# Fused sigmoid attention and MLP mixer on one core: tile 2 of two lots kept and done together with the next lot's, by seven products

## The chip, the cores and the metric

The kernel runs on one core of a Trainium2 chip. The time is device microseconds of one execution: the median of the runs of the kernel before is 340.74 us (three runs, 340.58 to 341.35). The engines are named as in the profile: PE is TensorE (matmuls), PEld its weight loads, DVE is VectorE, ACT is ScalarE, POOL is GpSimd, SP is SyncE, which here issues DMAs.

## The reference

```python
# q, k, v: (8, 12, 448, 64) float32; S = 448
scores = (1 / sqrt(64)) * q @ k.transpose(0, 1, 3, 2) - log(S)
attn = 1 / (1 + exp(-scores)) @ v                  # per batch and head
x = attn.transpose(0, 2, 1, 3).reshape(8, 448, 768)
xt = x.transpose(0, 2, 1)
u = x + (relu(xt @ w_tok1) @ w_tok2).transpose(0, 2, 1)   # w_tok1 (448, 256)
out = u + relu(u @ w_ch1) @ w_ch2                          # w_ch1 (768, 1536)
```

Four pieces follow each other for each of the eight batches: attention, the token mixer (448 to 256 to 448), the first channel product (768 to 1536) and the second one (1536 to 768).

## The kernel before, in words

**Stages.** Work is written out by hand in one order (`manual_schedule`: nothing is moved), three batches deep. A cycle is one batch `b` and one unit `u` of four heads, so three cycles make a batch. In the steady part (`steady`, b = 3 to 7) a cycle holds the seven score tiles of (b, u) (`qk`, L187: PE writes one of two PSUM buffers, ACT takes the sigmoid, L194), attention times values of the cycle before (`av`, L218), the token mixer of the cycle before that (`tok_tail` L277, `tok1` L296, `ytrans` L316), and pieces of the second channel product of `lot = b - 2`. At the end of u = 2 stands the whole first channel product of batch b - 1 (`sevens`, L516), on which ACT and DVE work as well.

**Array modes.** Scores, values and the "split" products run the array as four 64x64 quarters; `tok1`, `ytrans`, `sevens` and the "plain" products run it whole (128x128). In each cycle the 64x64 work comes first and one stretch of 128x128 work ends it.

**Seven products.** Tiles are 128 tokens: tiles 0, 1, 2 of a lot are whole, tile 3 has 64 tokens. `ch2_seven` does two tiles by Strassen's seven products over halves of the contraction and of the output columns, each of six blocks of 128 (a block is one 128x128 matmul of 384 columns, or one step of four 64x64 ones). Products 1, 6, 7, 4 pile up in that order in one PSUM bank, 2 in a second, 5 and 3 in a third tile that has the second one's bank. After each product its `end` (L843, DVE) adds the bank into an output tile, so a product that goes on in a bank waits for the `end` of the one before it there. Sums of weights that the products need are made by DVE (`sums`, L803). The output is stored by SP after products 3 (first tile) and 4 (second).

**Who does what, before.** u = 0: products 1 and 2 split (`two_jobs`), 6 and 5 plain. u = 1: 7 and 3 split, 4 plain. u = 2: tile 3 as a split (`last_split`, L671), then tile 2 alone (`ch2_pair`, 24 blocks: 14 split at L387 and 10 plain at L652), then `sevens`. A run that is split in two turns has a DVE copy of one element (`turn_over`, L854) between the turns.

**Banks and buffers.** PSUM banks 0 and 1 ("Y") are used in turn by `av`, `tok_tail`/`tok1` and `ytrans`, banks 2 and 3 ("X") by the lot's products; each use waits until DVE or ACT has emptied the bank. DVE empties `av` by two casts (L227), `ytrans` by two adds into `xu` (L326). The SBUF tag `parts` is a ring of four buffers that holds the outputs of tiles 0 and 1 and the six ACT copies of `sevens` (`pt_ab` and `pt_c`, L537) in the order in which they are asked for; a copy into a buffer that held an output waits until that output is stored. `h2` (the hidden layer), `diffs`, `outs`, `raw_q`, `rel_k` and `rel_q` have one buffer each, `un` (u, tokens first) two.

**Token sums and relayouts.** `token_sums(b - 1)` (four DVE instructions, L459) makes the sums that `sevens` uses from its fifth step on. `through_dma` gives eight pieces for the next batch's k and q: three DVE copies (L129) and one DMA transpose on SP (L142), for k and then for q; `some(n)` does the next n of them, (0, 1) in u = 0 (`within`, `behind`), (3, 4) in u = 1. `utrans` (L343) is one more DMA transpose on SP, at the end of u = 1. `gated_loads` lets POOL wait for the q transpose and then load.

Of the kernel before, what the change touches and what calls it, by code (L numbers as in the profile page):

```python
# [9 lines left out]
FP16 = mybir.dt.float16  # L10
FP32 = mybir.dt.float32
# [10 lines left out]
NJ = 7  # L22
NP = 64
NU = 3
# [6 lines left out]
def kernel(  # L31
# [11 lines left out]
    nc = tc.nc  # L43

    B, H, S, E = q.shape
# [4 lines left out]
    NCB = CC // 128  # L50
# [216 lines left out]
    def tok_tail(b, u):  # L267

        h1_tile(b, u)
        tks[b] = [  # L270
            bank([128, 2, 2, 128], FP32, f"tk_{b}_{u}_{tcb}")[:, 0, :, :]
            for tcb in range(2)
        ]
        for tcb in range(2):
            part = slice(64 * tcb, 64 * tcb + 64)
            for g in range(2):
                nc.tensor.matmul(  # L277
                    out=tks[b][tcb][64 * g : 64 * g + 64],
                    lhsT=w1[part, 3, 128 * tcb + 64 * g : 128 * tcb + 64 * g + 64],
                    rhs=xn[b, u][part, :, 3, :],  # L280
                    start=True,
                    stop=False,
                )
# [177 lines left out]
    def ch1_seven(b, banks):  # L461
# [93 lines left out]
    outs = {}  # L555
    orow = out.rearrange("b (p j) d -> b j p d", j=NJ)

    AT_END = {
        (B - 2, 0): "raw_k",
        (B - 2, 1): "raw_q",  # L560
# [5 lines left out]
    def out_tile(b, t):  # L566
        if b == 0 and t < 2:
            outs[b, t] = out_0[:, D * t : D * t + D]
            return
        tag, bufs = ("outs", 1) if t == 2 else ("parts", 4)  # L570
        if (b, t) in AT_END:
            tag, bufs = AT_END[b, t], 2 if AT_END[b, t] == "raw_v" else 1
        outs[b, t] = pa.tile([128, D], FP32, tag=tag, bufs=bufs, name=f"o_{b}_{t}")
# [188 lines left out]
    class ch2_seven:  # L762

        CHAIN = {1: "X", 6: "X", 7: "X", 4: "X", 2: "Y", 5: "Z", 3: "Z"}

        def __init__(self, rows, sides, X, Y, Z, at_end=True):
            self.rows, self.ps, self.banks = rows, {}, {"X": X, "Y": Y, "Z": Z}
            b = rows[1][0]
            tag, bufs = ("tr_k", 2) if at_end else ("diffs", 1)
            hid = pa.tile(  # L770
                [128, 3, NCB // 2, 128], FP16, tag=tag, bufs=bufs, name=f"hid_{b}"
            )
            self.held = {n: hid[:, at, :, :] for at, n in enumerate((5, 6, 7))}
            if at_end:
                hid3 = pa.tile(
                    [128, NCB // 2, 128], FP16, tag="tr_q", bufs=2, name=f"hid3_{b}"
                )
                self.held[3] = hid3[:, :, :]
            (self.a11, self.a12), (self.a21, self.a22) = [
                (side[:, LOW, :], side[:, HIGH, :]) for side in sides  # L780
            ]
            self.held.setdefault(3, self.a12)
            self.weights = {1: self.a11, 2: self.a12, 4: self.a22}
            self.moving = {
                1: c2[:, LOW, D1],
                2: c2[:, HIGH, D1],
                3: c2[:, HIGH, D2],
                5: hsums[0],
                6: hsums[1],
                7: hsums[2],  # L790
                4: hsums[3],
            }
# [43 lines left out]
        def end(self, n):  # L836
            row, half = {1: (0, 0), 2: (0, 0), 6: (0, 1), 3: (0, 1)}.get(n, (1, int(n != 4)))
            b, t = self.rows[row]
            if (b, t) not in outs:
                out_tile(b, t)  # L840
            o = outs[b, t][:, DH * half : DH * half + DH].rearrange("s (u d) -> s u d", d=128)
            opens = n in (1, 6, 5, 4)
            nc.vector.tensor_tensor(  # L843
                out=o,
                in0=un[b][:, :, half, t, :] if opens else o,
                in1=self.ps[self.CHAIN[n]][:, 0:DH].rearrange("s (u d) -> s u d", d=128),
                op=ADD,
            )
            if n in (3, 4):
                store(b, t)  # L850

    def turn_over(ps):

        nc.vector.tensor_copy(out=turned[:, :], in_=ps[:, 0:1])  # L854

    def two_jobs(jobs):

        def step(turn, n):
            for r in range(2):
                ps, lhsT, rhs, opens, end = jobs[r ^ turn]  # L860
                part = slice(64 * r, 64 * r + 64)
                for m in (0, 64):
                    nc.tensor.matmul(  # L863
                        out=ps[m : m + 64, 0:DH],
                        lhsT=lhsT(n)[part, m : m + 64],
                        rhs=rhs(n)[part, :],
                        start=(opens and turn == 0 and n == 0),
                        stop=(turn == 1 and n == NCB // 2 - 1),
                        skip_group_check=True,
                    )  # L870

        def end():
            for job in jobs:
                job[-1]()

        turns = [
            [lambda t=t, n=n: step(t, n) for n in range(NCB // 2)] for t in range(2)
        ]
        return turns[0], lambda: turn_over(jobs[1][0]), turns[1], end
# [335 lines left out]
    def some(n):  # L1215
        for f in copies[:n]:
            f()
        del copies[:n]
# [83 lines left out]
    def more(n):  # L1302
        for f in extra[:n]:
            f()
        del extra[:n]
# [5 lines left out]
    def score(n=1):  # L1311
        for _ in range(n):
            qk(*next(scores))

    def steady(b, u):

        lot, before, ahead = b - 2, divmod(NU * b + u - 1, NU), divmod(NU * b + u - 2, NU)
        within, behind = (
            ((0, 0), (4, 2), (2, 0)) if b == NU else ((0, 1), (3, 4), (0, 0))
        )[u]  # L1320

        def run(steps, n):
            for f in steps[:n]:
                f()
            del steps[:n]

        at_bank[0] = X
        if u < 2:
            if u == 0:
                sides = [h2[lot][:, :, 128 * t : 128 * t + 128] for t in range(2)]  # L1330
                sevenfold[lot] = ch2_seven(
                    [(lot, 0), (lot, 1)], sides, X, X + 1, X + 1, at_end=False
                )
                sevenfold[lot].sums(0, 2)
            more((0, 3)[u])
            seven = sevenfold[lot]
            turn0, turn, turn1, end = two_jobs([seven.job(n) for n in ((1, 2), (7, 3))[u]])
            score(2)
            run(turn0, 6)
            turn()  # L1340
            at_bank[0] = Y
            av(*before, 0, 1)
            score()
            av(*before, 1, 5)
            score()
            av(*before, 5, NJ)
            xtrans_dma(*before)
            run(turn1, 2)
            score()
            run(turn1, 4)  # L1350
            end()
            if u == 0:
                if b + 1 < B:
                    nc.gpsimd.tensor_copy(out=gate[:, :], in_=outs[lot, 0][:, 0:2])
                    load(b + 1, "q", q, 0, NU)
                seven.sums(2, 4)
                more(1)
            score()
            some(within)
            at_bank[0] = Y  # L1360
            tok_tail(*ahead)
            tok1(*ahead, with_scores=True)
            for n in ((6, 5), (4,))[u]:
                seven.plain(n)
        else:
            ps = [bank([128, 512], FP32, f"c2_{lot}_3_{r}") for r in range(2)]
            steps, end = last_split(lot, ps)
            score(2)
            run(steps, 7)
            score()  # L1370
            run(steps, 5)
            send = end(put_off=True)
            some(within)
            score()
            at_bank[0] = Y
            av(*before, 0, 5)
            score()
            at_bank[0] = X
            turn0, turn1, rest = ch2_pair(lot, u, 7, loose=True)
            run(turn0, 3)  # L1380
            score()
            run(turn0, 4)
            turn_over(turn_bank[0])
            av(*before, 5, NJ)
            xtrans_dma(*before)
            send()
            token_sums(b - 1)
            score()
            run(turn1, 2)
            score()  # L1390
            run(turn1, 5)
            at_bank[0] = Y
            tok_tail(*ahead)
            score()
            tok1(*ahead, with_scores=True)
            rest()
            sevens(b - 1)
        at_bank[0] = Y
        ytrans(*ahead)
        if u == 1:  # L1400
            utrans(b - 1)
        some(behind)
        if u == (2 if b == NU else 1) and b < B - 1:
            gated_loads(b)

    for c in range(ONE_RUN, N_CYCLES):
# [100 lines left out]
```

## Time and profile before

| what | value |
|---|---|
| median of the runs | 340.74 us |
| the profiled execution, whole | 340.27 us |
| its span | 338.5 us |
| PE busy, share of the span | 332.2 us, 98% |
| DVE busy | 235.3 us, 70% |
| ACT busy | 212.7 us, 63% |
| one batch of the steady part (138.9 to 177.3 us, 177.3 to 215.6 us) | 38.4 and 38.3 us |

The profiled execution lies 0.47 us under the median; 1.77 us of it lie outside the span. A row of the timeline gives the start (us from the span's start), the time from the first start to the last end, the engine, the line, the operation, what it writes and reads, the shape and how many alike follow each other. A PE matmul's own duration is longer than the time until the next may start, so the pace is read from starts. For a DMA that SP issues, the row's duration is the time for which SP is taken by the issue, not the time until the data has landed.

### The profile page before, as it was taken

How to read it: one execution, taken by the hardware profiler on the slowest of the kernel's cores; microseconds unless marked ns; L12 is line 12 of the kernel's file. 1: busy time of each engine (PE TensorE's matmuls, PEld its weight loads, DVE VectorE, ACT ScalarE, POOL GpSimd, SP SyncE). 2: the span in 40 equal slices, each digit the busy share in tenths (PEclk: the TensorE clock that was granted, in tenths of full speed). 3: DMA queues.
4: the chain of work that ended last, by engine and by line, in shares of the span. 5: the costliest groups of instructions: out<-in, count | busy, mean ns of one | idle time of the engine just before them, and what ended most of it. 6: DMA issues, size and time to landing. Idle time of an engine off the chain costs nothing.

```text
span 338.5 us, 10318 instructions
## 1 busy us (share of the span) xinstructions
PE 332.2 (98%) x4436; PEld 242.9 (72%) x4436; DVE 235.3 (70%) x486; ACT 212.7 (63%) x272; POOL 61.7 (18%) x108
## 2 busy tenths in 40 slices
PE   8999999999999999999999999999999999999994
PEld 5655556555896679767896679766896679769852
DVE  2376466678998874877668774877768653976882
ACT  4996845388747885678647885678657895314200
POOL 8985380050031002020032001110010000000000
PEclk9999999999999999999999999999999999999999
DMA  8999999999999899989998899988993393028006
GB/s 128 162 160 202 207 178 203 175 175 234 186 179 194 158 171 203 182 125 179 186 190 133 152 151 215 201 123 163 195 179 65 67 171 85 2 56 186 4 13 196
DMA packets 103422, 51.91 MB, mean 153 GB/s; under 512 B 75473, under 2 KB 100305, under 8 KB 103377
## 3 DMA queue, kind: packets, MB, share of 16 engines
q1 hardware_dynamic: 77648, 28.84, 47.0%
q0 software_dynamic: 25264, 21.50, 42.4%
q10 hardware_dynamic: 464, 0.92, 1.0%
q8 instruction: 34, 0.56, 0.6%
q14 instruction: 12, 0.09, 0.1%
HBM read 43.45 MB, written 11.01 MB: 161 GB/s over the span
## 4 chain that ended last, share of the span: by engine, by line
PE 81%; DMA 11%; POOL 5%; DVE 1%; issue 1%; ACT 0%; ACTq 0%; POOLq 0%
PE c_ab L516 14%; PE c L816 10%; PE c_c L516 8%; PE qk L187 8%; PE xa L218 7%; PE c L863 6%; DMA raw_k<-in_k_dram 5%; PE tk L296 4%; PE yt L316 4%; PE c L586 4%; PE c L387 4%; DMA raw_v<-in_v_dram 3%; PE c L671 3%; DMA c<-in_moe_w_ch_dram 3%; PE c L652 2%; POOL raw_q L118 2%
## 5 line engine op out<-in xcount | busy, mean ns | idle before, releaser
L194 ACT ACTIVATE att<-qk,att_bias 128x896 f16<-128x896 f32 x168 | 155.9, 1012 | 37.8 <-PE qk L187 36.7
L187 PE MATMUL qk<-tr_q,tr_k 64*64 64x448 f16 x672 | 60.8, 357 | 0.3 <-DVE tr_k L179 0.2
L516 PEld LDWEIGHTS <-c 128*128 128x128 f16 x504 | 48.4, 98 | 1.1 <-issue 0.3
L218 PE MATMUL xa<-att,raw_v 64*64 64x448 f16 x644 | 40.6, 349 | 0.0
L187 PEld LDWEIGHTS <-tr_k 64*64 64x64 f16 x672 | 25.3, 104 | 18.7 <-issue 11.5
L516 PEld LDWEIGHTS <-sum 128*128 128x128 f16 x378 | 36.3, 98 | 0.0
L227 DVE CAST xu<-xa 128x448 f16<-128x448 f32 x40 | 23.1, 619 | 18.3 <-PE xa L218 17.9
L537 ACT ACTIVATE pt_ab<-c_ab 128x896 f32<-128x896 f32 x21 | 19.2, 917 | 20.6 <-PE c_ab L516 20.6
L218 PEld LDWEIGHTS <-raw_v 64*64 64x64 f16 x672 | 21.9, 107 | 8.2 <-issue 0.4
L863 PE MATMUL c<-c,h 64*64 64x384 f16 x360 | 24.6, 323 | 0.0
L1136 POOL COPY gate<-tr_q 128x2 f16<-128x2 f16 x6 | 1.1, 184 | 121.9 <-DMA tr_q<-rel_q 121.9
L326 DVE TENSOR_TENSOR xu<-xu,yt 128x448 f16<-128x448 f16 x38 | 21.8, 615 | 0.0
L539 ACT ACTIVATE h<-c_ab 128x896 f16<-128x896 f32 x7 | 6.4, 917 | 24.4 <-PE c_ab L516 24.4
L296 PE MATMUL tk<-xn,w 128*128 128x256 f16 x156 | 21.2, 274 | 0.1
L546 DVE TENSOR_TENSOR h<-pt_ab,c_ab 128x896 f16<-128x896 f32 x14 | 15.2, 1083 | 8.6 <-PE c_ab L516 8.6
L546 DVE TENSOR_TENSOR h<-pt_c,c_c 128x448 f16<-128x448 f32 x21 | 12.9, 616 | 11.7 <-PE c_c L516 11.6
L310 ACT ACTIVATE h<-tk 128x256 f16<-128x256 f32 x42 | 14.2, 405 | 9.9 <-PE tk L296 9.9
L316 PE MATMUL yt<-w,h 128*128 128x448 f16 x88 | 20.3, 353 | 0.0
L843 DVE TENSOR_TENSOR o<-un,c 128x384 f32<-128x384 f16 x32 | 17.4, 551 | 4.0 <-PE c L816 4.0
L816 PEld LDWEIGHTS <-hid 128*128 128x128 f16 x132 | 12.9, 98 | 8.0
L516 PE MATMUL c_ab<-diffs,c 128*128 128x224 f16 x168 | 18.4, 259 | 0.0
L118 POOL DMA_DIRECT2D raw_k<-in_k_dram x26 | 16.8, 661 | 8.0 <-DMA c<-in_moe_w_ch_dram 5.6
(132 smaller groups left out, 574.4 us busy)
## 6 DMA issues: line engine op xcount, KB each, us to landing
out_dram<-o SPq DMA_DIRECT2D x41, 192.0 KB, 3.3
c<-in_moe_w_ch_dram POOLq DMA_DIRECT2D x3, 1152.0 KB, 11.6
raw_k<-in_k_dram POOLq DMA_DIRECT2D x10, 336.0 KB, 6.6
raw_q<-in_q_dram POOLq DMA_DIRECT2D x10, 336.0 KB, 5.6
raw_v<-in_v_dram POOLq DMA_DIRECT2D x10, 336.0 KB, 8.2
raw_q<-in_q_dram POOLq DMA_DIRECT2D x16, 112.0 KB, 5.9
raw_k<-in_k_dram POOLq DMA_DIRECT2D x16, 112.0 KB, 6.9
out_dram<-o SPq DMA_DIRECT2D x15, 96.0 KB, 2.4
```

Source lines behind the costliest of these rows:

```text
L118: nc.gpsimd.dma_start(out=dst.rearrange("p u hi j e -> p (u hi) (j e)"), in_=heads.rearrange("h (p j) e -> p h (j e)", j=NJ),)
L187: nc.tensor.matmul(out=ps[64 * g : 64 * g + 64, hi, 0:S], lhsT=tr[b, "k"][64 * hi : 64 * hi + 64, u, j, 64 * g : 64 * g + 64], rhs=tr[b, " ...
L194: nc.scalar.activation(out=att[b, u, j][:, :, :], in_=ps[:, :, 0:S], func=SIGMOID, bias=bias_t[:, :], scale=att_scale,)
L218: nc.tensor.matmul(out=ps[g][64 * hi : 64 * hi + 64, 0:S], lhsT=raw[b, "v"][64 * g : 64 * g + 64, u, hi, j, :], rhs=att[b, u, j][64 * g : ...
L227: nc.vector.tensor_copy(out=xu(b)[:, u, g, 0:S], in_=ps[g][:, 0:S])
L296: nc.tensor.matmul(out=ps[tcb], lhsT=w1[rows, t, cols], rhs=xn[b, u][rows, :, t, :], start=(t == 0 and not with_scores), stop=(t == (2 if ...
L316: nc.tensor.matmul(out=ps[:, 0:S], lhsT=h1[b, u][:, tcb, g, :], rhs=w2[:, tcb, :, :], start=(tcb == 0), stop=(tcb == 1),)
L326: nc.vector.tensor_tensor(out=x, in0=x, in1=ps[:, 0:S], op=ADD)
L516: nc.tensor.matmul(out=ps[:, g, p, :], lhsT=weights[n][:, d, 128 * cb : 128 * cb + 128], rhs=moving[n][:, d, :], start=(n in (1, 5, 2) and ...
L546: nc.vector.tensor_tensor(out=shaped(dst), in0=shaped(parts[gs, which]), in1=ps, op=ADD)
L816: nc.tensor.matmul(out=ps[:, 0:DH], lhsT=self.weights[n][:, k, :], rhs=self.moving[n][:, k, :], start=(n in (1, 2, 5) and k == 0), stop=(k ...
L863: nc.tensor.matmul(out=ps[m : m + 64, 0:DH], lhsT=lhsT(n)[part, m : m + 64], rhs=rhs(n)[part, :], start=(opens and turn == 0 and n == 0), ...
```

## The change

For lots 2 and 4 (worked on in b = 4 and b = 6; "late") tile 2 is not done. Its hidden values and its piece of `un` are copied aside by DVE (`late`, `un_late`), and one batch later (b = 5 and b = 7; "paired") it is done together with tile 2 of lots 3 and 5 by seven products in place of `ch2_pair`.

- In a late batch the seven products of tiles 0 and 1 are dealt out anew: u = 0 has 1 and 2 split and 6 plain; u = 1 has 5 and 7 split, with `tok_tail` and `tok1` put into the second turn after two of its six steps; u = 2 has 3 and 4 split, ahead of tile 3 and of the values. The `within` and `behind` counts become (0, 1), (3, 1), and three pieces in u = 2 after the turn; `gated_loads` moves to u = 2. `token_sums` stays ahead of tile 3.
- In a paired batch u = 2 has two `sums` ahead of tile 3, then products 1 and 2 split, two more `sums`, 6 plain, `token_sums`, and 5, 7, 3, 4 plain. The sums are kept in `h2` itself.
- The two outputs of the pair lie in `raw_q` and `rel_k`, not in `outs` or the ring.

```diff
+    LATE_TILE = {4: 2, 6: 4}
+    PAIRED = {b + 1: lot for b, lot in LATE_TILE.items()}
...
+        if t == 2 and late:
+            tag, bufs = "raw_q" if b in LATE_TILE.values() else "rel_k", 1
...
+    def late_pair(lot):
+        free = h2[lot]
+        return ch2_seven(
+            [(PAIRED[lot + 2], 2), (lot, 2)],
+            [h2[PAIRED[lot + 2], "late"], free[:, :, 256:384]],
+            X,
+            X + 1,
+            X + 1,
+            at_end=False,
+            held={
+                5: free[:, LOW, 0:128],
+                6: free[:, HIGH, 0:128],
+                7: free[:, LOW, 128:256],
+                3: free[:, HIGH, 128:256],
+            },
+        )
...
+        if b in LATE_TILE:
+            within, behind = ((0, 1), (3, 1), (0, 0))[u]
...
-            turn0, turn, turn1, end = two_jobs([seven.job(n) for n in ((1, 2), (7, 3))[u]])
+            pair = ((1, 2), (5, 7) if b in LATE_TILE else (7, 3))[u]
+            turn0, turn, turn1, end = two_jobs([seven.job(n) for n in pair])
...
             run(turn1, 2)
             score()
+            split_run = u == 1 and b in LATE_TILE
+            if split_run:
+                at_bank[0] = Y
+                tok_tail(*ahead)
+                tok1(*ahead, with_scores=True)
             run(turn1, 4)
+            if split_run:
+                score()
             end()
...
-            for n in ((6, 5), (4,))[u]:
+            for n in ((6,), ())[u] if b in LATE_TILE else ((6, 5), (4,))[u]:
                 seven.plain(n)
+        elif b in LATE_TILE:
+            turn0, turn, turn1, end = two_jobs([sevenfold[lot].job(n) for n in (3, 4)])
+            score(2)
+            run(turn0, 6)
+            turn()
+            some(3)
+            at_bank[0] = Y
+            av(*before, 0, 2)
+            score()
+            run(turn1, 4)
+            score()
+            run(turn1, 2)
+            end()
+            av(*before, 2, 5)
+            score()
+            av(*before, 5, NJ)
+            xtrans_dma(*before)
+            token_sums(b - 1)
+            at_bank[0] = X
+            ps = [bank([128, 512], FP32, f"c2_{lot}_3_{r}") for r in range(2)]
+            steps, end = last_split(lot, ps)
+            run(steps, 4)
+            score()
+            run(steps, 3)
+            score()
+            run(steps, 3)
+            score()
+            run(steps, 2)
+            end()
+            late = pa.tile([128, NCB, 128], FP16, tag="outs", bufs=1, name=f"late_{lot}")
+            nc.vector.tensor_copy(out=late[:, :, :], in_=h2[lot][:, :, 256:384])
...
+            nc.vector.tensor_copy(out=un_late[lot][:, :, :, :], in_=un[lot][:, :, :, 2, :])
+            h2[lot, "late"] = late
             at_bank[0] = Y
             tok_tail(*ahead)
+            score()
             tok1(*ahead, with_scores=True)
+            sevens(b - 1)
         else:
+            both = late_pair(lot) if b in PAIRED else None
+            if both:
+                both.sums(0, 2)
...
             run(turn1, 5)
+            if both:
+                end()
+                both.sums(2, 4)
             at_bank[0] = Y
             tok_tail(*ahead)
             score()
             tok1(*ahead, with_scores=True)
-            rest()
+            if both:
+                both.plain(6)
+                token_sums(b - 1)
+                for n in (5, 7, 3, 4):
+                    both.plain(n)
+            else:
+                rest()
             sevens(b - 1)
...
-        if u == (2 if b == NU else 1) and b < B - 1:
+        if u == (2 if b == NU or b in LATE_TILE else 1) and b < B - 1:
             gated_loads(b)
```

## The prediction on record

> **What bounds the kernel now.** I read the page's busy lines first, then the stretches of one batch each, then PE's timeline through b = 4, then DVE, SP and ACT at the places that the change touches.
>
> ```profile
> PE 332.2 (98%) x4436; PEld 242.9 (72%) x4436; DVE 235.3 (70%) x486; ACT 212.7 (63%) x272; POOL 61.7 (18%) x108
> ```
> ```profile
> 138.90:177.30 38.40, 38.40 (x566) 29.92 (x564) 27.70 (x59) 26.92 (x36) 4.50 (x8) 1.00 1.02 175
> ...
> 330.00:338.50 8.50, 3.94 (x41) 2.35 (x39) 2.01 (x4) 0.48 (x1) 0.00 (x0) 0.90 0.70 196
> ```
>
> PE has no gap in a batch (38.40 of 38.40 us), so each matmul less is time, and each wait of PE is time too. PE timeline, u = 1 of b = 4 and on:
>
> ```profile
> 151.51 0.36 PE L187 MATMUL qk<-tr_q,tr_k 64*64 64x448 f16 x4
> 151.70 0.36 PE L277 MATMUL tk<-xn,w 64*64 64x256 f16 x4
> 151.99 0.83 PE L296 MATMUL tk<-xn,w 128*128 128x256 f16 x6
> 152.65 1.14 PE L816 MATMUL c<-hsum_b,h 128*128 128x384 f16 x6
> 153.63 0.92 PE L316 MATMUL yt<-w,h 128*128 128x448 f16 x4
> 154.48 0.57 PE L187 MATMUL qk<-tr_q,tr_k 64*64 64x448 f16 x8
> ...
> 162.84 1.79 PE L652 MATMUL c<-c,h 128*128 128x384 f16 x10
> 164.46 1.31 PE L516 MATMUL c_ab<-xu,c 128*128 128x224 f16 x12
> ```
>
> Paces from starts: a block is 0.162 us ((164.46 - 162.84)/10), a set of scores 0.19. The tail L277 takes 0.11, then PE waits 0.12 before the whole array starts; after `ytrans` (four at 0.19) it waits 0.10 for the quarters: a pair of mode changes is 0.22. DVE in the same place:
>
> ```profile
> 150.55 1.16 DVE L227 CAST xu<-xa 128x448 f16<-128x448 f32 x2 [1.53 <-PE xa L218]
> 151.74 0.20 DVE L233 COPY xu<-xu 128x128 f16<-128x128 f16 x1
> 151.85 1.01 DVE L843 TENSOR_TENSOR o<-o,c 128x384 f32<-128x384 f32 x2
> 152.78 1.14 DVE L129 COPY rel_k<-raw_k 128x896 f16<-128x896 f16 x2
> ```
>
> The casts free banks 0 and 1 at 151.2 and 151.71, and the tail, which takes these banks, starts at 151.70: PE arrives just as they come free. That is the picture at many places here: the waits are there, with almost no slack.
>
> **The parts.** Sums are per pair of batches (one late, one paired); there are two pairs.
>
> (1) *Blocks.* Before: 42 (seven products) + 12 (tile 3) + 24 (tile 2) = 78 per lot, 156 per pair. After: 54 in the late batch, 96 in the paired one, 150. Six blocks less: -0.97. The late batch alone loses 24 (-3.89), the paired one gains 18 (+2.92).
>
> (2) *Modes.* `tok1` stands in the middle of the second turn in late u = 1, between quarters: one pair of changes more, +0.22.
>
> (3) *Tail ahead of its banks.* In late u = 1 the tail comes four steps (0.65) and a score (0.19) earlier, the casts do not: PE waits +0.84.
>
> (4) *DVE's queue, late u = 2.* Count from the tail's start. Tail, change, `tok1` (0.66), change, four steps: product 5 is done on PE at 1.63 and on DVE's side at 1.83. `end` 5 and `end` 7 (0.60 and 0.47, as two dependent L843 rows are spaced) and two relayouts (0.53 each) stand ahead of the `ytrans` adds, which free bank 0 at 4.56 and bank 1 at 5.10. PE meanwhile: score 0.19, change 0.12, `ytrans` 0.76, change 0.10, two scores, six steps 0.98: it wants bank 0 for `av` at 4.25 and waits 0.9 for both. Behind the adds DVE still has the `utrans` copy and a relayout (0.7) before the one-element copy between the turns; PE gets to its second turn about 0.5 before that is done. Together +1.4. Three scores then stand 0.68 apart (three steps and a score) while ACT takes about 0.89 for each sigmoid and there are two PSUM buffers: 0 to +0.6, I take +0.4.
>
> (5) *SP's queue and the ring.* This is the largest step.
>
> ```profile
> 153.33 1.19 SPq L623 DMA_DIRECT2D out_dram<-o  x2
> 154.61 3.97 SPq L142 DMA_TRANSPOSE tr_k<-rel_k  x1
> 158.68 1.22 SPq L623 DMA_DIRECT2D out_dram<-o  x2
> 159.99 4.62 SPq L343 DMA_TRANSPOSE un<-xu  x1
> 164.72 3.80 SPq L142 DMA_TRANSPOSE tr_q<-rel_q  x1
> ```
> ```profile
> 168.74 0.92 ACT L537 ACTIVATE pt_ab<-c_ab 128x896 f32<-128x896 f32 x1 [0.66 <-PE c_ab L516]
> 169.84 0.92 ACT L537 ACTIVATE pt_ab<-c_ab 128x896 f32<-128x896 f32 x1 [0.18 <-PE c_ab L516]
> ```
>
> SP issues in order, and a transpose holds it for 3.8 to 4.6 us. Before, tile 0's output is stored ahead of all three transposes (153.33) and tile 1's at 158.68. After, products 3 and 4 are done in u = 2, so both stores stand behind tr_k, un and tr_q. On before's clock: tr_k's relayouts are done at 154.8 (late u = 0 is 0.97 shorter), then 3.97 + 4.62 + 3.80 and some 0.1 between: the first store is issued at 167.4, its second half at 168.0, and it lands 3.4 later (the page's median for these stores is 3.3): 171.4. The ring's four buffers hold outputs 0 and 1 and two copies, so the third copy of `sevens` (the first `pt_ab` row above) takes output 0's buffer: done at 172.4. PE wants to go on in that bank with product 7, which before starts at 171.36 and now at 170.3 (all terms so far: -0.97 -0.97 -1.95 +0.22 +0.84 +1.4 +0.4). PE waits 2.1, and about 0.4 more for the smaller bank, as the next copy waits for output 1's store and ACT is in order: +2.5. Bounds: no wait if the stores landed 2 us sooner than their row; single landings in this trace run from 2.7 to 7.4 us, so up to +4 more.
>
> (6) *Sums ahead of tile 3, paired u = 2.*
>
> ```profile
> 193.94 1.66 DVE L129 COPY rel_q<-raw_q 128x896 f16<-128x896 f16 x3
> 195.57 0.56 DVE L709 TENSOR_TENSOR o<-un,c 128x384 f32<-128x384 f16 x1
> 196.24 0.56 DVE L715 TENSOR_TENSOR o<-o,c 128x384 f32<-128x384 f32 x1
> ```
>
> DVE goes from the relayouts straight to tile 3's adds; the next product's second matmul starts on PE at 196.84, 0.04 after the second add. Two sums (L803, a pair takes 1.06 in u = 0) go in between: +1.06. In b = 7 there is no next batch, so no relayouts (1.66), and the sums fit: 0.
>
> (7) *Product 3 behind `token_sums`, paired.* Product 6 ends on PE; 0.2 later its `end` (0.47), then four token sums (2.0: the L459 rows run from 199.92 to 201.93), then `end` 5 (0.55): bank free 3.25 after product 6. PE needs 1.95 for products 5 and 7, then 3 waits for that bank: +1.25.
>
> (8) *What costs nothing.* The two copies of DVE (0.6 to 1.0 for 1536 columns, by the rates of a 128x896 scalar operation at 0.39 and a relayout) stand where DVE sits 1.5 us idle ahead of `sevens`' first add; without that cover up to 0.5. The next values' transpose on SP is 1.3 later, 10 us before its use. `gated_loads` waits for tr_q in both kernels, which lands no later. Three more `end`s per pair are in (4) and (7).
>
> Sum: first pair -0.97 +0.22 +0.84 +1.4 +0.4 +2.5 +1.06 +1.25 = +6.7; second, without (6), +5.6. 340.27 + 12.3 = **352.6 us**; the profiled execution lies 0.47 under the median, within the runs' own spread (0.77), so I add nothing.
>
> **The rivals.** *The ring does not bind* (stores land early or their queue moves faster): 352.6 - 5.0 = 347.6. For it: a landing 2 us shorter is enough. Against: three transposes in a row are fixed, 12.4 us. 0.13.
>
> *The other side: shorter batches.* PE's gain shows because each bank is free when PE comes; it decides at the 0.84 of (3): if `av` ended that much sooner for DVE, then the queue behind it would be too. Price: 2 x (-0.97 + 0.22) = 338.8. Against: PE and DVE are in step to 0.06 us there already, and nothing in the change moves the casts ahead. 0.05.
>
> *The clock drops.* The granted clock is 1.00 where PE has no gap and 0.90 in the last 8.5 us, where PE is busy for 3.94. If the stores take 5.1 us, the wait of (5) grows by 1.7 per pair to about 3.8, and if PE then ran the 6.0 us that are left of `sevens` at less, say 3 us more per pair, it would be 352.6 + 3.4 + 6 = 362. Against: 2.1 is no long gap. 0.06. [...]
>
> *The change is not what it says*: the listing of instructions has 36 matmuls fewer and the order above; no chance for that.
>
> **How the numbers follow.** The forecast has 0.75, with its own range 349 to 358 (ring +-3 to the late side, 4 and 7 fairly sure); the early ring 0.13, the other side 0.05, the clock 0.06, no change 0.01. The range 347.2 to 358 takes in the early ring and late landings in both pairs. Less than 0.2% (0.7 us) is about what cannot be told from no change: faster 0.05, same 0.01, slower 0.94.
>
> **What would show it.** Right: PE idle of 0.8 before L277 in u = 1 of b = 4 and 6; idle before `av` in u = 2; 2 us or more before product 7 of `sevens` with ACT as the releaser and a store behind it; about 1.2 before product 3 in b = 5 and 7; b = 4 longer than 38.4 and b = 6 alike. Wrong: `sevens` without a gap in b = 4, or the values' banks free in time.

## The result and the profile after

The changed kernel takes 355.72 us (median of six runs, 352.56 to 359.2) against 340.66 us: 1.041 times the time before, 95% interval 1.036 to 1.046. Ratios here leave out executions more than 1.5% above the fastest of their kernel (one of these six). Its profiled execution is the fastest of them, 352.56 us with a span of 350.8; the forecast for it was 352.6.

The busy line of its page, and the stretches of batches 4, 5 and 6 (each up to the next batch's first score; the first one starts 0.18 us ahead of its own, which is at 139.10; columns: from:to, length, then busy us of PE, PEld, DVE, ACT and POOL, the granted clock, the DMA share and GB/s):

```profile
PE 335.7 (96%) x4400; PEld 240.2 (68%) x4400; DVE 244.7 (70%) x504; ACT 213.6 (61%) x272; POOL 62.0 (18%) x108
```
```profile
138.92:178.71 39.79, 36.88 (x538) 26.96 (x537) 27.99 (x60) 27.25 (x36) 4.50 (x8) 1.00 1.01 164
178.71:222.23 43.52, 41.83 (x577) 31.60 (x576) 32.25 (x68) 26.97 (x35) 4.53 (x8) 1.00 0.96 171
222.23:261.83 39.60, 36.70 (x535) 26.96 (x534) 27.71 (x60) 27.18 (x35) 3.21 (x6) 1.00 0.86 138
```

Batch 5 in the kernel before:

```profile
177.39:215.70 38.31, 38.31 (x566) 29.91 (x565) 27.62 (x60) 26.84 (x35) 4.60 (x8) 1.00 1.01 166
```

The 36 matmuls are gone (4436 to 4400). The late batches, which lost 24 blocks, are not shorter than before (38.3 us from first score to first score) but 1.3 longer (39.6), with 2.9 us of gaps on PE; the paired batch is 5.2 longer, of which 18 blocks explain 2.9. The clock is 1.00 in all of them: in this execution the loss is waits.

Where they stand, by PE's timeline. First late u = 1 and u = 2 of b = 4:

```profile
149.72 0.36 PE L187 MATMUL qk<-tr_q,tr_k 64*64 64x448 f16 x4
150.28 0.30 PE L277 MATMUL tk<-xn,w 64*64 64x256 f16 x2 [0.20 <-DVE xu L227]
150.81 0.30 PE L277 MATMUL tk<-xn,w 64*64 64x256 f16 x2 [0.23 <-DVE xu L227]
...
156.00 0.57 PE L218 MATMUL xa<-att,raw_v 64*64 64x448 f16 x6 [0.16 <-DVE xu L326]
```

Read the starts, not the idle time in brackets, which counts from the modelled end of a longer matmul: after the score at 149.72 (0.19) the tail could start at 149.91. Its first pair waits 0.37 for the first cast, its second 0.47 for the second. In u = 2 the values' second bank waits for the second `ytrans` add in the same way (last row).

Then `sevens` of b = 4, on PE, ACT and SP:

```profile
169.18 1.31 PE L516 MATMUL c_c<-diffs,sum 128*128 128x224 f16 x12
172.29 1.31 PE L516 MATMUL c_ab<-diffs,c 128*128 128x224 f16 x12 [1.80 <-ACT pt_ab L537]
```
```profile
171.32 0.92 ACT L537 ACTIVATE pt_ab<-c_ab 128x896 f32<-128x896 f32 x1 [4.27 <-DMA out_dram<-o]
```
```profile
154.91 3.17 SPq L142 DMA_TRANSPOSE tr_k<-rel_k  x1
158.14 4.49 SPq L343 DMA_TRANSPOSE un<-xu  x1
162.73 3.27 SPq L142 DMA_TRANSPOSE tr_q<-rel_q  x1
166.10 2.47 SPq L630 DMA_DIRECT2D out_dram<-o  x4
```

This is one chain read backwards: product 7 waits for ACT's copy, the copy 4.27 us for a store's landing, and the four store pieces stand behind three transposes on SP. Before, the same copy waited for PE alone.

Last the paired batch: DVE ahead of tile 3's first add, then DVE and PE at product 3:

```profile
197.40 0.56 DVE L812 TENSOR_TENSOR h<-h,late 128x768 f16<-128x768 f16 x1
197.88 0.55 DVE L716 TENSOR_TENSOR o<-un,c 128x384 f32<-128x384 f16 x1
```
```profile
204.84 0.92 DVE L459 TENSOR_TENSOR diffs<-xu 128x672 f16<-128x672 f16 x2
...
206.76 0.55 DVE L853 TENSOR_TENSOR o<-un,c 128x384 f32<-128x384 f16 x1
```
```profile
207.36 1.14 PE L825 MATMUL c<-c,h 128*128 128x384 f16 x6 [1.08 <-DVE o L853]
```

Tile 3's adds stand behind the sums, and product 3 waits for an `end` (206.76) that stands behind four token sums (from 204.84 on).

### The profile page after: what moved, and what is told of

Read it like the earlier page. It is cut to its first block, busy times and chain, and to the rows that moved or that the text cites. A ratio compares the mean times of both kernels' runs of the same rounds, so it can differ in the third digit from the quotient of the medians.

```text
span 350.8 us, 10266 instructions
## 1 busy us (share of the span) xinstructions
PE 335.7 (96%) x4400; PEld 240.2 (68%) x4400; DVE 244.7 (70%) x504; ACT 213.6 (61%) x272; POOL 62.0 (18%) x108
## 4 chain that ended last, share of the span: by engine, by line
PE 77%; DVE 10%; ACT 5%; DMA 4%; issue 2%; SPq 1%; DVEq 0%; ACTq 0%
PE c_ab L516 12%; PE c L825 10%; PE qk L187 9%; PE xa L218 8%; PE c L873 7%; PE c_c L516 7%; PE tk L296 5%; ACT att L194 4%; PE yt L316 4%; PE c L593 3%; DMA out_dram<-o 2%; PE c L364 2%; PE c L387 2%; DVE o L853 2%; PE c L678 2%
## 5 line engine op out<-in xcount | busy, mean ns | idle before, releaser
L187 PE MATMUL qk<-tr_q,tr_k 64*64 64x448 f16 x672 | 60.0, 357 | 0.5 <-DVE tr_k L179 0.2
L218 PE MATMUL xa<-att,raw_v 64*64 64x448 f16 x644 | 41.5, 349 | 0.6 <-DVE xu L326 0.5
L853 DVE TENSOR_TENSOR o<-un,c 128x384 f32<-128x384 f16 x36 | 19.6, 550 | 7.6 <-PE c L825 4.1
L853 DVE TENSOR_TENSOR o<-o,c 128x384 f32<-128x384 f32 x30 | 16.3, 552 | 4.0 <-PE c L825 2.6
L825 PEld LDWEIGHTS <-h 128*128 128x128 f16 x120 | 11.6, 98 | 9.9 <-issue 2.9
```

The source lines that it names most:

```text
L187: nc.tensor.matmul(out=ps[64 * g : 64 * g + 64, hi, 0:S], lhsT=tr[b, "k"][64 * hi : 64 * hi + 64, u, j, 64 * g : 64 * g + 64], rhs=tr[b, " ...
L218: nc.tensor.matmul(out=ps[g][64 * hi : 64 * hi + 64, 0:S], lhsT=raw[b, "v"][64 * g : 64 * g + 64, u, hi, j, :], rhs=att[b, u, j][64 * g : ...
L825: nc.tensor.matmul(out=ps[:, 0:DH], lhsT=self.weights[n][:, k, :], rhs=self.moving[n][:, k, :], start=(n in (1, 2, 5) and k == 0), stop=(k ...
L853: nc.vector.tensor_tensor(out=o, in0=u if opens else o, in1=self.ps[self.CHAIN[n]][:, 0:DH].rearrange("s (u d) -> s u d", d=128), op=ADD,)
```

## The experiments

The theory: the forecast's waits, each a term of its own, make the time; the work itself is shorter. Rivals: the stores are late for another reason; the waits hide each other, so that undoing one gives nothing; and the granted clock, since the six executions after run from a clock of .999 (352.56 us) down to .983 (359.2 us), while those before stay within 1 us.

**1. SP's order.** Late batches only:

```diff
-            some(3)
+            some(2)
...
             end()
+            utrans(b - 1)
+            some(1)
             av(*before, 2, 5)
...
-        if u == 1:
+        if u == 1 and b not in LATE_TILE:
             utrans(b - 1)
```

> The changed kernel, but in late batches SP issues the values' transpose and the q transpose behind the stores of tiles 0 and 1 (only tr_k ahead of them, as in the kernel before, where it is one of three). Nothing else moves. Theory: the wait at product 7 of sevens in b = 4 and 6 (shift of 2.35 and 2.26 us in the trace, and a part of it on the way) is SP's three transposes in a row ahead of the stores, so both waits are gone: 352.56 - 4.6 = 348.0 for the profiled execution. Rival 1: the stores land late for another reason (their landing time, DMA traffic): no change, 352.6. Second question: the executions of the changed kernel run from 352.6 to 359.2 us with a granted clock of .999 down to .983. If the clock is lost because PE waits about 2 us in each of these places, all executions here have .997 or more and lie within 1 us; if it is another matter, the spread of 4 to 6 us stays.

347.66 us (347.39 to 347.71, five runs), 1.020 times before (1.019 to 1.021). SP and PE of it in b = 4:

```profile
158.78 2.89 SPq L630 DMA_DIRECT2D out_dram<-o  x4
161.77 4.22 SPq L343 DMA_TRANSPOSE un<-xu  x1
```
```profile
170.25 1.31 PE L516 MATMUL c_ab<-diffs,c 128*128 128x224 f16 x12
```

The stores are issued ahead of the values' transpose, 7.3 us sooner, and product 7 starts 1.15 after the product before it, without a wait. Rival 1 is out. The spread is gone as well: 0.32 us, the clock .997 or more. So whatever spreads the changed kernel's executions hangs on this wait.

**2. The paired batches' two waits**, first the token sums alone, then both, each on top of 1:

```diff
-                both.plain(6)
+                for n in (6, 5, 7):
+                    both.plain(n)
                 token_sums(b - 1)
-                for n in (5, 7, 3, 4):
+                for n in (3, 4):
                     both.plain(n)
```
```diff
-            if both:
-                both.sums(0, 2)
             ps = [bank([128, 512], FP32, f"c2_{lot}_3_{r}") for r in range(2)]
...
             send = end(put_off=True)
+            if both:
+                both.sums(0, 2)
```

> The changed kernel with the mended SP queue of the late batches (347.7) and the token sums of the paired batches behind product 7 in place of product 6; the two sums stay ahead of tile 3. Tells the two waits of the paired batches apart. Theory: product 3's wait (1.2 in each of two batches) goes, the sums' wait (1.0, in b = 5 alone) stays: 347.7 - 2.4 = 345.2. Rival: the sums' place is the larger of the two, then it stays at 346.5 or more.

> The run above, and in paired batches the first two sums behind tile 3's adds and the token sums behind product 7 in place of product 6. Theory: both waits of the paired batches go (about 1.0 once, in b = 5, and 1.2 in each of two batches): 348.0 - 1.0 - 2.4 = 344.6. Rival: the sums of weights are late for product 1 in their new place, or the token sums for step 5 of sevens, and the time comes back: 348.

The token sums alone: 345.58 us, 1.0148 (1.0130 to 1.0166). Both: 344.17 us, 1.0100 (1.0085 to 1.0114). By the traces (PE's start of the same matmul against before) the paired batch b = 5 costs 4.24 us beyond its sums' wait (0.98) in the changed kernel, and 3.00 in all with both edits: 2.92 of it are the 18 blocks. So product 3's wait was 1.24. With the token sums alone mended, b = 5 costs 3.98, which leaves 0.98 for the sums. The terms add up.

**3. The tail back behind both turns**, on top of 2, and then alone on the changed kernel:

```diff
-            split_run = u == 1 and b in LATE_TILE
+            split_run = False
```

> The run above, and the late batches' u = 1 does not split the second turn: tail and tok1 stand behind both turns as in the kernel before. Theory: one pair of mode changes (0.22), the wait ahead of the tail (0.84) and the later start of DVE's queue in u = 2 (1.4) go in each late batch, but ytrans then follows tok1 at once and waits for its ReLU (0.8): 344.6 - 2 x (2.46 - 0.8) = 341.3, about as long as before (340.3). Rival: DVE's queue is what counts in u = 2 and only starts later, so that the mode change and the 0.84 alone go and the ReLU's wait takes it back: 344.

> The changed kernel with one part undone: the late batches' u = 1 does not split the second turn (tail and tok1 stand behind both turns). The ring, the sums and the token sums stay as they are. With the mended SP queue the same edit brought 344.2 to 341.8, 2.3 us. Theory: SP's chain starts with the k relayouts, which DVE also does earlier without the split turn, so the stores come earlier too and the waits add: the profiled execution at a full clock is 352.6 - 2.3 to 3.3 = 349.3 to 350.3. Rival: what is won ahead of the ring is lost at the ring, as the stores stand behind 12.4 us of transposes: PE waits as much longer there, 352.6 at a full clock.

On top of 2: 341.83 us, 1.0027 (1.0016 to 1.0037); 2.3 us less, where 3.3 were expected. Its PE waits 0.7 for the ReLU ahead of `ytrans` in each late batch. The waits ahead of the tail, the values' banks and the second turn are gone from its rows; those at two scores of late u = 2 (0.17 and 0.22) and ahead of tile 3 (0.19) stand as in the changed kernel, so they did not come from the tail's place. Alone: 351.61 us (350.68 to 354.65), 1.033 (1.030 to 1.037), and 350.68 for the profiled execution. Here both sides had a part: by the traces each late batch is 1.4 to 1.5 shorter up to `sevens`; in b = 4 the ring's wait is a little shorter too (2.05, was 2.35), in b = 6 it takes 0.9 of the gain back (3.15, was 2.26).

**4. The ring alone, in the kernel before.** No product moves; the stores of tiles 0 and 1 of lots 2 and 4 are only issued later:

```diff
-            if n in (3, 4):
+            if n in (3, 4) and not (b in (2, 4) and t < 2):
                 store(b, t)
...
             xtrans_dma(*before)
+            if lot in (2, 4):
+                store(lot, 0)
+                store(lot, 1)
             send()
```

> The kernel before, with one thing changed: for lots 2 and 4 (b = 4 and 6) the stores of tiles 0 and 1 are issued only in u = 2, behind the transposes of k, values and q and ahead of tile 3's stores. No product, sum or mode moves. Theory: the ring alone makes PE wait ahead of product 7 of sevens, with ACT's third copy as the releaser; the first store is then issued at about 168.6, lands 3.4 later, the copy ends at 173.0 and PE, which wants to go on at 171.4, waits 1.5 to 2: plus 2 x 1.5 to 2.5 = 343.5 to 345.5, and no gap elsewhere. Rival: the ring does not bind and what was lost in the changed kernel is lost by late products: 340.7. If waits of 1.5 to 2 us lower the granted clock, some executions here lie 2 us or more above the lowest at a clock under .995; if not, all lie within 1 us.

352.5 us (347.95 to 356.03), 1.030 (1.026 to 1.035), clock .974 to .992: the place was right (in its trace nothing but the two `sevens` of b = 4 and 6 is longer, by 5.2 and 8.5 us), the size three times too small. ACT and PE in b = 4:

```profile
174.90 0.92 ACT L537 ACTIVATE pt_ab<-c_ab 128x896 f32<-128x896 f32 x1 [2.97 <-DMA out_dram<-o]
```
```profile
176.30 1.28 PE L516 MATMUL c_c<-diffs,c 128*128 128x224 f16 x6 [3.01 <-ACT pt_c L537]
```

The trace has two reasons for the size. In b = 4 the pieces issued up to 168.6 landed in 2.9 to 3.9 us; those issued after 169.1, when POOL's gated loads start, took 5.5 to 8.5. And the clock fell. The stretches of 1 us behind the gaps in b = 4 and in b = 6 (the clock is the number after the five busy times):

```profile
175.00:176.00 1.00, 0.00 (x0) 0.00 (x0) 0.15 (x1) 1.00 (x2) 0.00 (x0) 0.92 1.19 195
176.00:177.00 1.00, 0.70 (x5) 0.56 (x5) 0.97 (x2) 0.68 (x2) 0.00 (x0) 0.50 1.20 230
...
179.00:180.00 1.00, 1.00 (x11) 0.93 (x10) 0.36 (x1) 0.00 (x0) 0.00 (x0) 0.88 1.26 223
```
```profile
257.00:258.00 1.00, 0.83 (x8) 0.78 (x8) 0.00 (x0) 0.12 (x1) 0.00 (x0) 0.88 1.08 362
...
264.00:265.00 1.00, 1.00 (x10) 0.85 (x8) 0.21 (x1) 0.00 (x0) 0.00 (x0) 0.71 0.00 0
```

Between the edge rows every stretch has 0.50. Twelve matmuls that start at 177.37 take 2.1 us in place of 1.15.

**5. Each reason by itself, on top of 4.** The loads gated on something later, and spare matmuls in the gap:

```diff
-        nc.gpsimd.tensor_copy(
-            out=gate[:, :], in_=tr[b + 1, "q"][:, NU - 1, NJ - 1, 126:128]
-        )
+        late = h2[b - 1][:, 4, 0:2] if b in (4, 6) else tr[b + 1, "q"][:, NU - 1, NJ - 1, 126:128]
+        nc.gpsimd.tensor_copy(out=gate[:, :], in_=late)
...
-        if u == (2 if b == NU else 1) and b < B - 1:
+        if u == (2 if b in (NU, 4, 6) else 1) and b < B - 1:
```
```diff
+            if b in (3, 5) and n == 7:
+                at_bank[0] = 1
+                spare = bank([128, 512], FP32, f"spare_{b}_{gs}")
+                for _ in range(16):
+                    nc.tensor.matmul(
+                        out=spare[:, 0:256], lhsT=c1[:, 0, 0:128], rhs=c1[:, 0, 0:256],
+                        start=True, stop=True,
+                    )
             step(n, gs)
```

> The kernel before with the stores of tiles 0 and 1 of lots 2 and 4 held back as in the earlier run, and one thing more: in b = 4 and 6 the loads that POOL issues as soon as the q transpose has landed wait for a later thing (a piece of the hidden layer, done some 2.5 us later). There the run with the held stores gave 347.9 to 356 us; its stores issued before those loads landed in 2.9 to 3.9 us, the ones behind them in 5.5 to 8.5. Theory: it is the loads that make these stores late; without them all eight pieces land in 3 to 4 us, PE waits 1.5 to 2 in each batch and the time is 343.5 to 345.5 with a granted clock over .995 throughout. Rival: the stores queue behind each other whatever else is on its way: no change, 348 to 356, and some executions under .99.

> The kernel before with the held stores, and 16 spare matmuls of 256 columns (0.11 us each, 1.75 us) ahead of product 7 of sevens in b = 4 and 6, for the large bank and again for the small one, whose result nothing reads. PE then works through the first 1.75 us of each wait. The earlier run's profile has waits of 3.0 and 3.8 us, and from 0.7 us before or after their end on a granted clock of 0.50 for 3.3 and 6.6 us. Theory: the clock falls because PE stands idle; with no gap over 2 us it stays: all executions over .995, the time is that of the late stores alone, about 347 to 349, and lies within 2 us. Rival: the clock falls for another reason (transfers, current): executions at .98 to .99 and 350 to 356 as before.

Later loads: 343.67 us (342.75 to 346.29), 1.0091 (1.0063 to 1.0119); the eight pieces of b = 4 land in 2.2 to 3.4 us, and five of six executions have a clock of .996 or more (the one at 346.29 has .991). Spare matmuls: 348.23 us (347.46 to 349.2), 1.0220 (1.0201 to 1.0239), clock .997 or more. So by the medians the ring and SP's order alone cost 3 us, the clock some 4 (352.5 to 348.2) and the collision with the loads the other 4.6 (348.2 to 343.7). The collision also makes the gaps in which the clock falls: with later loads it stays in five of six executions. The median of 4 comes from another chip than the two of 5, so the parts are rough.

**6. Is it the same in the changed kernel?** Once more without an edit; with the spare matmuls, ahead of product 7's large bank only; and with the loads gated later. The first has no diff, the other two are those of 5, on top of the changed kernel (where the loads already stand in u = 2), but for one line in the spare matmuls:

```diff
-            if b in (3, 5) and n == 7:
+            if b in (3, 5) and (n, gs) == (7, "ab"):
```

> The changed kernel once more, unchanged, for its spread (352.6 to 359.2 us at a granted clock of .999 to .983). The run with held stores showed the clock fall to 0.50 for 3.4 us after a gap of 3.0 us on PE. Theory: here the same happens in some executions, when the stores land a little later than in the profiled one (gap of 1.8 us, clock 1.00): times again spread over 3 us or more, the longer the lower the clock, and if the profiled execution is one of these, its trace shows 0.50 in the stretch behind the gap in sevens of b = 4 or 6 and nowhere else in the steady part. Rival: the spread belonged to the chip of that day: all within 1 us of 352.7.

> The changed kernel with 16 spare matmuls of 256 columns (1.75 us) ahead of product 7 of sevens for the large bank in b = 4 and 6, whose result nothing reads: PE works through most of the wait of 1.8 us that the profile shows there. Theory: the wait is not shorter, but the clock stays: all executions at .995 or more and within 1.5 us of 352.6, which is 2 us or more under the median of the changed kernel (355.7). Rival: the clock falls for another reason: spread and median as without the spare matmuls, or 3 us more where the spare work is not covered.

> The changed kernel, but in b = 4 and 6 POOL's loads of the next batches wait for a piece of the hidden layer that is done about 2.5 us after the q transpose has landed. In the changed kernel's profile these loads are issued from 168.5, just behind the four stores (166.1 to 168.0), which then take 3.3, 4.5, 4.2 and 4.4 us to land; spare matmuls in the wait kept the clock at .995 or more, and yet the executions there ran from 351.7 to 357.1. Theory: what varies from execution to execution is the landing of the stores, as they share the transfer engines with these loads. Without them the stores land in 3 to 3.3 us, the ring's wait falls by about 1 us in each of two batches, to 350 to 351, and the executions lie within 1.5 us. Rival: the landing varies anyway, the loads only happen to stand beside it: 352.6 or more at the lowest and a spread of 3 us or more.

Again: 353.42 us (352.83 to 355.65), clock 1.000 to .992, the longest at .992; the profiled execution (352.84) has no stretch under 1.00 in `sevens`, so the fall itself was not caught in this kernel. Spare matmuls: 353.23 us (351.65 to 357.06). The clock stays at .995 or more, as expected, but the spread is there all the same: the expected 1.5 us is refuted, and the clock is not the main cause of the spread. Later loads: 351.84 us (351.21 to 352.35), 1.031 (1.028 to 1.034): the spread falls to 1.1 us, as the landing theory had it; it was measured on another chip than the two runs before, so the chip's part in that is not excluded. The lowest time did not fall as far as expected: the wait is 2.0 and 1.7 us (was 2.35 and 2.26), and three of the four pieces in b = 4 still take 4.0 to 4.3 us, although POOL's first load starts only at 171.4, when the first of these three lands. What delays them is open.

**7. A version with the waits covered.** From 2, without the split second turn as in 3, and with the late batches' order written anew (`late` here is u = 1 of a late batch; its `ytrans` moves behind the next two scores). The core of the edit:

```diff
             av(*before, 1, 5)
+            if late:
+                av(*before, 5, NJ)
             score()
-            av(*before, 5, NJ)
+            if not late:
+                av(*before, 5, NJ)
             xtrans_dma(*before)
-            run(turn1, 2)
+            run(turn1, 3 if late else 2)
             score()
...
             score(2)
-            run(turn0, 6)
+            at_bank[0] = Y
+            ytrans(*divmod(NU * b + u - 3, NU))
+            run(turn0, 3)
+            score()
+            run(turn0, 3)
             turn()
-            some(2)
+            some(1)
...
             utrans(b - 1)
-            some(1)
+            some(3)
```

> The changed kernel with the mended SP queue, sums and token sums, and the late batches' hand-written order made anew: the tail stands behind both turns as before the change, one score comes after the values and not before them, ytrans stands behind the next two scores (which cover the ReLU at the price of one pair of mode changes), the q relayouts come behind ytrans' adds, and the scores of u = 2 are spread so that ACT has one sigmoid every 0.9 us. Theory: the work itself is shorter than before (six blocks per pair, -0.97) and all that made the change slow are waits of its order; with none left but the mode changes (0.22 per pair) it is 2 x (-0.97 + 0.22) = -1.5 against before: 339.3. Rival: the late batches cannot be that short, since ACT's sigmoids are too dense there (7 in each unit at 0.9), and 1 us or more comes back: 340.5 to 342, like the version with the mended tail (341.8).

339.42 us (339.16 to 340.18, six runs), 0.9962 times before (0.9949 to 0.9975): 0.4% less than before, a small gain but clear of the noise. Its busy line has PE at 98% of a shorter span again:

```profile
PE 330.5 (98%) x4400; PEld 239.2 (71%) x4400; DVE 243.0 (72%) x504; ACT 213.0 (63%) x272; POOL 61.7 (18%) x108
```

By the traces each late batch is 3.60 us shorter than before (24 blocks less a pair of mode changes are 3.67) and each paired one 3.00 longer. Two late and two paired batches make 2 x (-3.60 + 3.00) = -1.2, which is the difference of the medians (339.42 and 340.60). ACT was not too dense. Buffers of their own for the outputs, which would have taken the ring out of the question, were not tried.

## Why the prediction was right, and where it was only partly so

The mechanism was right: waits on PE at the forecast places outweigh the blocks saved. By PE's starts the first pair of batches is 6.5 us longer than before (forecast 6.7) and the second 5.5 (5.6). That the profiled execution came within 0.1 us of 352.6 is luck: it is the fastest of six that run up to 359.2, and inside the terms errors cancel.

- **(1) Blocks:** shown. The version with nothing else left in it has -3.60 and +3.00 per batch, forecast -3.89 + 0.22 and +2.92.
- **(1) to (4), the late batch up to `sevens`:** forecast -1.03 in sum; the trace has -1.05 in b = 4 and -0.97 in b = 6. The 0.84 of (3) is 0.37 + 0.47 in the rows above. That (2), (3) and the DVE queue of (4) hang on the tail's new place is shown by run 3: with the tail back, 2.3 us for two batches, with the ReLU's wait taking a part back. Their separate sizes are read from one trace only. In its rows of b = 4 the 1.4 of (4) is about 1.1 (0.7 at the values' banks, where the forecast had 0.9, and 0.4 at the second turn), the 0.4 for the scores is 0.4 (0.17 and 0.22), and 0.2 stands ahead of tile 3, which the forecast did not have: the sum is as close as it is because these errors nearly cancel.
- **(5) The ring:** forecast +2.5 per pair, measured 2.35 and 2.26; removed by SP's order (run 1) and made without any other part of the change (run 4). The issue was forecast for 167.4, and came at 166.1, as the transposes took 10.9 us together and not 12.4, which the prediction had called fixed; the landing took 4.5 for the first output's second half, not 3.4. Two errors of opposite sign: the mechanism held, the size of the wait was hit by luck.
- **(6) Sums ahead of tile 3:** +1.06 forecast, 0.98 in the trace of b = 5, none in b = 7.
- **(7) Product 3:** +1.25 forecast, 1.24.
- **(8) The copies:** 0.56 and 0.35 us, and DVE still idles 1.20 behind them. Nothing, as forecast.
- **The clock rival** (0.06, 362 us) was set too low. The fall is real in the held-store kernel, and in executions of the changed kernel the clock goes down to .983. The profiled execution does not show it, and the forecast went by that kind of execution alone. That 2.1 us is no long gap and that a fall adds 3 us per pair were the author's estimates; no run shows the 3. What the runs showed: gaps of 1.8 us in the changed kernel and of 2.5 in run 3 left the clock at 1.00; in run 4, with gaps of 3.0 and 3.8 us, it was 0.50 for 3.4 and 6.8 us, and by the medians of runs 4 and 5 the clock cost some 4 us in both batches together. The median of the first six runs lies 3.1 us over it. What the forecast treated as one number, the landing (bounds up to +4 per pair in (5)), differs from one execution to the next.
- **The other side** (338.8, "shorter batches") was no description of this kernel, but nearly of run 7: 339.4. What it lacked was not an earlier cast; it was an order in which no wait stands.

## What to carry to other kernels

When work moves later, follow every DMA that it issues to its place in the issuing queue and from there to whoever waits for the buffer: a store behind three transposes cost more here (2.35 and 2.26 us in the two pairs) than six matmul blocks saved (0.97), and it was mended by two moved lines. Where PE has no gap before a change, write each new wait down as its own term: on one engine in order they added here nearly one by one, and could be undone one by one. A wait for a transfer was no constant here (192 KB stores of run 4 landed in 2.9 to 8.5 us): give it a spread, and ask what else starts at the same moment.

## What the runs showed of the hardware

**The clock.** In the profile of run 4 the edge rows give the moments: from 1.00 to 0.50 at 175.84 and 257.76, back at 179.24 and 264.58 (a row of mean 0.92 holds 0.84 us at 1.00 and 0.16 at 0.50). The low spells are 3.4 and 6.8 us. The first fall came 2.55 us after PE had stopped (173.29), within the gap of 3.0 us; the second 4.4 us after PE had stopped (253.34), when the gap of 3.8 us was over and PE had been working again for 0.59 us (from 257.17). Behind PE's last work the clock falls too: in the kernel before at 336.82, 2.9 us after it (333.95), in the changed kernel at 350.29, 4.3 us after it (346.00). So in these four falls the time from PE's stop was 2.5 to 4.4 us; no run here shows what sets it.

Shorter gaps left the clock at 1.00 in the profiled executions: in the changed kernel the longest one in `sevens` of b = 4 is 1.80 us (170.49 to 172.29) and of b = 6 1.49, and with the tail alone moved back (run 3) the longest wait is 2.5 us at a mean clock of 1.000. That later stores lengthen the gaps of other executions until the clock falls fits their clocks of .983 to .995, but no trace caught it.

**Transfers.** In b = 4 of run 4 a 192 KB store piece landed in 2.9 to 3.9 us when it was issued ahead of the four 336 KB loads and in 5.5 to 8.5 us behind their start; with the loads later, none of the pieces took over 3.4. What keeps pieces at 4.0 to 4.3 us where no such load runs (run 6) is not known.
